# A pre-norm attention and GEGLU block: attention output turned by DMA in bf16, GpSimd's maxima one step later, tangents held by a count, the last steps in pairs

## The chip, the cores and the metric

One core of one Trainium2 chip. The metric is device time in microseconds of one execution. A step-by-step profile of one execution gives the times of single instructions; it has its own time, which is told apart from the median of the runs.

## The reference

```python
x = A_x                                   # 1 x 2048 x 512, bf16
n = layernorm(x)                          # no scale, no shift, eps 1e-5
q, k, v = split(n @ wqkv)                 # 32 heads of 16
p = softmax(q @ k.T * 16 ** -0.5)         # per head, 2048 x 2048
h = x + concat_heads(p @ v) @ wo
m = layernorm(h)
out = h + (gelu_tanh(m @ w_gate) * (m @ w_up)) @ w_down      # F = 1792
```

## The kernel before

Everything is written out by a planner in Python that emits the instructions of each engine in a fixed order; semaphores let the engines run as far ahead as their data allow. Whatever the planner counts (steps, lags, budgets) shapes only that order. Nothing is decided on the chip.

**Units and steps.** The 2048 query rows are cut into 8 groups (`gi`) of 256 rows, the 32 heads into 8 slots of 4 heads. A unit (`ui`) is one group and one slot, so there are 64 (`NU`). Each unit takes 16 steps (`tick`). In a step the first pass (`p1_pair`, L797) computes two score tiles of 128 queries by 512 keys for two heads, and VectorE takes the row maxima of both in one instruction over 1024 columns (`p1_consume`, L806). The second pass runs 24 steps behind (`P2_START`): `p2_tile` (L867) computes the scores again, transposed, 256 keys by 256 queries in one bank, and ScalarE takes the exponential of each bank (`p2_consume`, L879), two in a step, into a ring `PT` of 34 tiles that lie in three tensors (23 in PTM, 4 in PTE, 7 in PTG). The score matmul uses 32 contraction rows of which 16 hold the head; three more rows carry minus the maximum, as three bf16 parts, so that no separate subtraction is needed.

**The maxima on GpSimd.** `negm_part` folds the maxima of key blocks 0 and 1 (at step 8 of a unit, L817 to L819) and of block 2 (at step 12, L821 to L824); `negm_pre` at step 15 folds the last (L832 to L834) and writes the three bf16 parts into ST (to L840). `negm_post` turns ST by a DMA transpose into STG (L846, on SP's queue), and `ADDX` = 4 steps later GpSimd adds STG to QT (L851). Only then may the unit's second pass begin.

**Dense work.** Beside the two passes, class `Dense` hands out pieces of other matmuls, one a step: projections, `item_pv`, `item_ofin`, `item_oproj`, `item_gate`, `item_up`, `item_down`. An item has a bank of its own while it runs; after it the stream pauses for `PAUSE` steps. Gate and up items start only if ScalarE's counted lag is under `LAG_START`. If a step has little dense work, `dummy` (L1285) adds matmuls on constants: two a step while the first pass runs, and up to `FILL_2` per two steps after it.

**Attention output.** `item_pv` (L893) multiplies the exponentials of a unit with V, which has a column of ones, so that 32-row blocks hold 16 outputs and their sum for each of 4 heads, by 256 queries. ScalarE evicts that to OA in fp32. After two units `item_ofin` turns both by four fp32 transposes on TensorE (L919), ScalarE evicts the result to OAT, and GpSimd takes the reciprocal of the sums by a power (`inv`, L928) and multiplies (`mul`, L932) into Otok. When all slots of a group are there, Otok is turned by DMA, projected with wo (`item_oproj`), normalised, turned by DMA again, and the group's FFN goes into the dense stream.

**FFN.** Seven pairs of gate and up items per group. Of the gate's result GpSimd makes the polynomial of the tanh form (L1062 to L1064), ScalarE the tangent (L1055, after `later` has seen a low enough lag), GpSimd the rest (L1060, L1061) and the product with the up part (L1114). `item_down` (L1122) then multiplies with w_down for each half of the group.

**GpSimd's order.** `PoolStream` holds the queued GpSimd work and hands it out within a budget of 1.19 us a step; what is emitted directly is charged by `spend`.

**The end.** After the last first-pass step, 24 second-pass steps remain. They are emitted two steps at a time, four tiles, one exponential for each, with evictions on VectorE (`dve_free`). `tail_a` and `tail_a2` project slots 0 to 5 of the last group in that stretch. `tail_b` then takes the last unit: `tail_norm`, `tail_onT`, the rest of the projection, layer norm, `tail_hnT`, and the FFN of the last group on TensorE, ScalarE and VectorE. `fill` keeps TensorE at work in between, with dense pieces (the down items of group 6 are kept back for it) or with dummies.

Of the kernel before, what the change touches and what calls it, by code (L numbers as in the profile page):

```python
# [222 lines left out]
ADDX = 4  # L223
# [3 lines left out]
FILL_2 = 4  # L227
FILL_LN = 16
LAG_START = 0.4
LAG_OP = 0.2  # L230
TANH_LAG = 2


def bass_sequential_preLN__mha_block__geglu_ffn__prompt_kernel(nc, A_x, A_wqkv, A_wo, B_x, B_w_gate, B_w_up, B_w_down, out):
    dbg = None
    with ExitStack() as es:
# [74 lines left out]
        OAT = at("OAT", [128, 2, 272], FP32)  # L311
# [189 lines left out]
        def startable(it, room):  # L501
            if it[0] is item_gate and par_busy[it[1][1] % 2] and room < 10:
                return False
            if it[0] is item_down and it[1][0] == GL - 1 and not force[0]:
                return False
            if it[0] is item_down and it[1][1] == 0 and not force[0]:
                return not gut_left.get(it[1][0], 0) and dense.now >= gut_last.get(it[1][0], 0) + 1
            return it[0] is not item_projT or not (qks_busy.get(("a", qk_n[0] % 4)) or qks_busy.get(("b", qk_n[0] % 2)))

        class Dense:  # L510
# [17 lines left out]
            def _start(self, item):  # L528
                genfn, a, est, nb = item
                if self.single:  # L530
                    self.bank = banks.take()
                else:
                    self.bank = self.banks[self.rr % len(self.banks)]
                    self.rr += 1
                self.gen = genfn(self.bank, *a)
            def piece(self):
                if self.single and self.pause > 0:
                    return 0
                while True:
# [11 lines left out]
                    try:  # L551
# [42 lines left out]
        class PoolStream:  # L594

            def __init__(self):
                self.q = []
                self.budget = 0.0
            def add(self, ops, then=None):
# [4 lines left out]
            def spend(self, cost):  # L604
                self.budget -= cost
            def run(self, flush=False):
                while self.q and (flush or self.budget >= min(self.q[0][0], 1.0)):
                    if not flush and self.q[0][0] > 2.0 and dense.now % 16 in (1, 2, 3, 13, 14, 15):
                        break
                    cost, fn, then = self.q.pop(0)  # L610
                    self.budget -= cost
                    fn()
# [229 lines left out]
        def negm_post(ui):  # L842
# [10 lines left out]
            defer(ADDX, add)  # L853
# [6 lines left out]
        def p2_tile(ui, j, gp, jj):  # L860
# [3 lines left out]
            m, g, b = j // 2, 2 * gp + jj, banks.take()  # L864
# [5 lines left out]
            return (b, m, g)  # L870

# [10 lines left out]
        def item_pv(b, ui):  # L882
# [18 lines left out]
            evac_act(OA[:, par, 256 * col:256 * col + 256], pbank[:, b, 0:256], [("pb", b)], [("OA", par, col)], cost=0.41)  # L901
            if gi == GL and slot >= NSLOT - 2:
                if col == 0:
                    dense.add(item_ofin, gi, (slot,), front=True, est=3, not_before=dense.now + 3)
            elif col == 1:
                dense.add(item_ofin, gi, (slot - 1, slot), front=True, est=3, not_before=dense.now + 3)
# [6 lines left out]
        oat_busy = {}  # L913
        def item_ofin(b, gi, slots):
            gp, par, ns = gi % 2, slots[0] // 2 % 2, len(slots)
            assert not oat_busy.get(par), "GpSimd too far behind"
            for q in range(2):
                for sp in range(ns):
                    P.op("pe", lambda e, q=q, sp=sp: e.transpose(out=pbank[:, b, 128 * (q * ns + sp):128 * (q * ns + sp) + 128], in_=OA[:, par, 256 * sp + 128 * q:256 * sp + 128 * q + 128], identity=ident32[:]),  # L919
                         reads=[("OA", par, sp), "ident32"], writes=[("pb", b)], sig=(q == 1 and sp == ns - 1))  # L920
                if q == 0 and ns == 2:
                    yield 1
            def norm():
                assert gi < 1 or otok_consumed.get(gi - 1), "dense stream too far behind (Otok reuse)"
                oat4 = OAT[:, par, 0:136 * ns].rearrange("p (q h i) -> p q h i", q=2, i=17)
                li = LINV[:, par, 0:8 * ns].rearrange("p (q h) -> p q h", q=2)
                def inv():
                    P.op("pool", lambda e: e.tensor_tensor(out=li, in0=oat4[:, :, :, 16], in1=negone[:, 0:8 * ns].rearrange("p (q h) -> p q h", q=2), op=ALU.pow),  # L928
                         reads=[("OAT", par), "negone"], writes=[("LINV", par)])
                o_ap = Otok[:, :, 64 * slots[0]:64 * slots[0] + 64 * ns].rearrange("p q (h i) -> p q h i", i=16)  # L930
                def mul():
                    P.op("pool", lambda e: e.tensor_tensor(out=o_ap, in0=oat4[:, :, :, 0:16], in1=li.unsqueeze(3).broadcast_to([128, 2, 4 * ns, 16]), op=ALU.mult),  # L932
                         reads=[("OAT", par), ("LINV", par)], writes=[("Otok", s_) for s_ in slots])
                oat_busy[par] = True
                def over():
                    oat_busy[par] = False
                    slot_done(gi, slots)
                pool.add([(1.45 * ns, inv), (0.31 * ns, mul)], then=over)
            v17 = lambda ap: ap.rearrange("p (qh i) -> p qh i", i=32)[:, :, 0:17]
            evac_act(OAT[:, par, 0:136 * ns].rearrange("p (qh i) -> p qh i", i=17), v17(pbank[:, b, 0:256 * ns]), [("pb", b)], [("OAT", par)], then=norm, cost=0.3)  # L940
            return 1

# [96 lines left out]

        gut_left = {}  # L1040
# [4 lines left out]
        def gelu_chain(par, dE):  # L1045
# [4 lines left out]
            def later(n):  # L1050
                if not force[0] and act_lag[0] > LAG_OP + 0.1 * n:
# [4 lines left out]
                defer(1, second)  # L1056
            def second():
                def done():
# [5 lines left out]
                      o(1.27, lambda e: e.tensor_tensor(out=ts_, in0=ts_, in1=gs, op=ALU.mult), [("th", par), ("g", par)])], then=lambda: defer(TANH_LAG, lambda: later(0)))  # L1064

        def gate_up_mms(b, gi, f, w, nm):
            hT = hnT_l[gi % 2]
            hr = [("hnT", gi % 2, k) for k in range(2)]
# [78 lines left out]
        def tail_a(b):  # L1147
# [9 lines left out]
            dense.add(tail_a2, front=True, est=4, not_before=dense.now + 2)  # L1157
            return 1

        def tail_a2(b):  # L1160
            gp = GL % 2
            for k in range(2):
                for hc in range(3):
                    P.op("pe", lambda e, k=k, hc=hc: e.matmul(pbank[:, k, :], OnT[:, k, hc, :], wo_sb[:, hc, :], start=(hc == 0), stop=False),
                         reads=[("OHa", 0), "wo"], writes=[("pb", k)], sig=False)
                    if hc == 1:
                        yield 2
                P.op("pe", lambda e, k=k: e.matmul(pbank[:, k, :], ident[:], g_h(GL, k), start=False, stop=False),
                     reads=["ident", ("h", gp, k)], writes=[("pb", k)], sig=(k == 1))
                if k == 0:  # L1170
                    yield 2
            a_done[0] = True
            return 2
        a_done = [False]
# [34 lines left out]
        def tail_hnT(b, k):  # L1209
            gp = GL % 2  # L1210
            pt = pbank[:, b, :].bitcast(BF16)
            for dc in range(4):
                P.op("pe", lambda e, dc=dc: e.transpose(out=pt[:, 128 * dc:128 * dc + 128], in_=hn_sb[:, k, 128 * dc:128 * dc + 128], identity=ident[:]),
                     reads=[("OH", k), "ident"], writes=[("pb", b)], sig=(dc == 3))
            o_ap = hnT_l[gp][:, :, 128 * k:128 * k + 128]
            i_ap = pt[:, 0:512].rearrange("p (c s) -> p c s", c=4)
            if k == 1:
                P.op("act", lambda e: e.activation(out=o_ap, in_=i_ap, func=ACT.Copy), reads=[("pb", b)], writes=[("hnT", gp, k)])
            else:
                P.op("dve", lambda e: e.tensor_copy(out=o_ap, in_=i_ap), reads=[("pb", b)], writes=[("hnT", gp, k)])  # L1220
# [6 lines left out]
        def tail_b():  # L1227
            P.op("act", lambda e: e.activation(out=htmp[:, 0:1], in_=nhalf[:, 0:1], func=ACT.Gelu_apprx_tanh), reads=["nhalf"], writes=[("htmp", 0)])
            fill(3)
            while not a_done[0]:  # L1230
                fill(1)
            in_bank(tail_norm)
            fill(3)
# [20 lines left out]
            for k in (0, 1):  # L1254
                in_bank(tail_hnT, k)
            fill(2)
# [6 lines left out]
            for k in range(2):  # L1263
                down_h(k, GL, k)
# [22 lines left out]

        p2_started = False
# [4 lines left out]
        while True:  # L1293
# [11 lines left out]
            dve_free[0] = not p1_ok  # L1305
            dense.tick(tick)
# [100 lines left out]
```

## Time and profile before

| what | us |
|---|---|
| median of 3 runs (lowest, highest) | 1243.94 (1243.86, 1244.21) |
| the profiled execution, its own time | 1243.15 |
| its span | 1241.4 |
| first maximum begins (L806) | 14.66 |
| last maximum begins (L806) | 1183.69 |
| last exponential ends (L879) | 1211.31 |
| last FFN's first gate matmul (L1072) | 1219.97 |

Granted clock of TensorE over the span: 0.997 of full speed. In a profile, PE is TensorE, PEld its weight loads, DVE VectorE, ACT ScalarE, POOL GpSimd, SP the queue that issues DMAs. A line of a group gives line, engine, operation, output and input tiles with shape and count, then the busy time in us, the mean of one in ns, and the idle time just before with what ended it. A line of a timeline gives start, length, engine, line, operation, tiles and how many were merged; in brackets the idle time before it. Instructions on ScalarE and VectorE overlap a little, so the distance from one start to the next (the pitch) is shorter than the duration of one.

Other groups that the change touches, of ScalarE and GpSimd, with shapes kept apart:

```profile
L641 ACT ACTIVATE OA<-pbank 128x256 f32<-128x256 f32 x62 | 24.8, 400 | 0.0
L641 ACT ACTIVATE OAT<-pbank 128x272 f32<-128x272 f32 x31 | 13.1, 422 | 0.0
L1055 ACT ACTIVATE th_sb<-th_sb 128x512 f32<-128x512 f32 x49 | 34.5, 704 | 1.4 <-POOL th_sb L1064 1.4
L851 POOL TENSOR_TENSOR QT<-QT,STG 128x256 bf16<-128x256 bf16 x64 | 42.8, 668 | 19.6 <-DMA STG<-ST 19.4
L821 POOL TENSOR_TENSOR MX<-PM,MX 128x8 f32<-128x8 f32 x64 | 13.0, 203 | 101.5 <-DVE PM L806 101.5
L832 POOL TENSOR_TENSOR MX<-PM,MX 128x8 f32<-128x8 f32 x64 | 12.9, 202 | 163.9 <-DVE PM L806 163.9
```

### The profile page before, as it was taken

The numbers are of one execution on the slowest core, as the hardware profiler recorded it, in microseconds if no ns is written. First come the engines' busy times: TensorE is split into PE (matmuls) and PEld (weight loads), VectorE is DVE, ScalarE is ACT, GpSimd is POOL, SyncE is SP. The second block draws the span as 40 slices with busy tenths as digits, with TensorE's granted clock in tenths as the row PEclk, the third lists the DMA queues.
The fourth block names the chain that finished last, engine by engine and source line by source line (L and its number), as shares of the span: only waits on it lengthen the run. The fifth ranks groups of instructions, "written<-read, shape, count | busy, mean of one in ns | idle before, by whom it ended". The sixth has DMA issues, their size and how long they took to land.

```text
span 1241.4 us, 31438 instructions
## 1 busy us (share of the span) xinstructions
PE 1137.8 (92%) x12680; PEld 437.8 (35%) x12680; DVE 1189.8 (96%) x1088; ACT 1199.9 (97%) x2464; POOL 764.3 (62%) x1540
## 2 busy tenths in 40 slices
PE   7999888899999999999999998999999999999998
PEld 3333222233333333333333333333333333333335
DVE  8999999999999999999999999999999999999923
ACT  7899999999999999999999999999999999999992
POOL 8647774467746765376645777367654766547760
PEclk9999999999999999999999999999999999999989
DMA  5101004300010000100010000100002000100000
GB/s 151 31 22 28 24 19 130 89 6 3 6 31 12 6 6 6 38 5 6 4 27 18 4 6 6 27 17 6 6 4 40 6 4 6 27 19 3 6 13 18
DMA packets 50800, 27.45 MB, mean 22 GB/s; under 512 B 36064, under 2 KB 49632, under 8 KB 50656
## 3 DMA queue, kind: packets, MB, share of 16 engines
q1 hardware_dynamic: 50656, 25.45, 8.0%
q8 instruction: 101, 1.65, 0.5%
q14 instruction: 43, 0.35, 0.1%
HBM read 11.80 MB, written 2.10 MB: 11 GB/s over the span
## 4 chain that ended last, share of the span: by engine, by line
DVE 58%; ACT 30%; PE 9%; POOL 2%; issue 1%; DMA 0%
DVE PM L806 57%; ACT PTM L879 17%; ACT PTG L879 5%; ACT PTE L879 3%; PE pbank L1122 2%; PE pbank L867 2%; PE pbank L797 1%; ACT th_sb L1055 1%; PE pbank L1072 1%; ACT g_sb L641 1%; ACT OnT L1012 1%; ACT u_sb L641 1%; PE pbank L739 1%; PE pbank L998 1%; PE pbank L676 1%
## 5 line engine op out<-in xcount | busy, mean ns | idle before, releaser
L806 DVE TENSOR_REDUCE PM<-pbank 128x2 f32<-128x1024 f32 x1024 | 1162.4, 1224 | 5.3 <-PE pbank L867 2.8
L879 ACT ACTIVATE PTM<-pbank 128x512 bf16<-128x512 f32 x1388 | 737.0, 669 | 4.7
L867 PE MATMUL pbank<-QT,KT 32*128 32x256 bf16 x4096 | 498.2, 273 | 9.7 <-ACT PTM L879 4.4
L797 PE MATMUL pbank<-KT,QT 32*128 32x512 bf16 x2048 | 394.2, 382 | 46.4 <-DVE PM L806 23.6
L1285 PE MATMUL pbank<-ones_bf,ident 128*128 128x512 bf16 x794 | 245.3, 384 | 28.1 <-ACT PTM L879 3.2
L797 PEld LDWEIGHTS pbank<-KT,QT 32*128 32x128 bf16 x2048 | 104.5, 91 | 392.7 <-DVE PM L806 170.3
L879 ACT ACTIVATE PTG<-pbank 128x512 bf16<-128x512 f32 x420 | 228.2, 660 | 1.1 <-PE pbank L867 0.3
L867 PEld LDWEIGHTS pbank<-QT,KT 32*128 32x128 bf16 x4096 | 164.5, 92 | 65.7 <-ACT PTM L879 36.8
L879 ACT ACTIVATE PTE<-pbank 128x512 bf16<-128x512 f32 x240 | 137.7, 667 | 1.9 <-PE pbank L867 1.1
L893 PE MATMUL pbank<-PTM,VA 128*17 128x256 bf16 x2776 | 125.8, 274 | 2.7 <-ACT PTM L879 1.2
L832 POOL TENSOR_TENSOR MX<-PM,MX 128x8 f32<-128x8 f32 x64 | 12.9, 202 | 163.9 <-DVE PM L806 163.9
L1285 PEld LDWEIGHTS pbank<-ones_bf,ident 128*128 128x128 bf16 x794 | 47.6, 97 | 131.4 <-ACT PTM L879 83.8
L928 POOL TENSOR_TENSOR LINV<-OAT,negone 128x16 f32<-128x16 f32 (+1 forms) x32 | 92.7, 2896 | 0.0
L893 PEld LDWEIGHTS pbank<-PTM,VA 128*17 128x17 bf16 x2776 | 60.1, 89 | 46.9 <-issue 29.1
L821 POOL TENSOR_TENSOR MX<-PM,MX 128x8 f32<-128x8 f32 x64 | 13.0, 203 | 101.5 <-DVE PM L806 101.5
L1072 PE MATMUL pbank<-hnT_l,wu_sb 128*128 128x256 bf16 x448 | 67.1, 276 | 3.1 <-ACT PTM L879 0.2
L1072 PE MATMUL pbank<-hnT_l,wg_sb 128*128 128x256 bf16 x448 | 66.9, 275 | 2.5
L1114 POOL TENSOR_TENSOR GUT<-th_sb,u_sb 128x512 bf16<-128x512 f32 x49 | 62.2, 1270 | 5.1 <-DVE u_sb L630 3.0
L1061 POOL TENSOR_TENSOR th_sb<-th_sb,g_sb 128x512 f32<-128x512 f32 x49 | 62.1, 1268 | 4.1
L1064 POOL TENSOR_TENSOR th_sb<-th_sb,g_sb 128x512 f32<-128x512 f32 x49 | 62.1, 1268 | 3.1
L1062 POOL TENSOR_TENSOR th_sb<-g_sb 128x512 f32<-128x512 f32 x49 | 51.0, 1041 | 18.8 <-ACT g_sb L641 18.8
L1122 PE MATMUL pbank<-wd_sb,GUT 128*128 128x512 bf16 x224 | 60.5, 382 | 0.6 <-ACT PTM L879 0.2
(149 smaller groups left out, 1077.3 us busy)
## 6 DMA issues: line engine op xcount, KB each, us to landing
QKS<-QKS SPq DMA_DIRECT2D x27, 112.0 KB, 2.2
x_sb<-in_A_x_dram SPq DMA_DIRECT2D x4, 512.0 KB, 5.6
xres<-in_A_x_dram SPq DMA_DIRECT2D x16, 128.0 KB, 2.2
out_dram<-out_sb SPq DMA_DIRECT2D x16, 128.0 KB, 1.8
wg_sb<-in_B_w_gate_dram SPq DMA_DIRECT2D x4, 448.0 KB, 5.0
wu_sb<-in_B_w_up_dram SPq DMA_DIRECT2D x4, 448.0 KB, 4.0
wd_sb<-in_B_w_down_dram SPq DMA_DIRECT2D x3, 512.0 KB, 6.4
STG<-ST SPq DMA_TRANSPOSE x64, 2.3
```

The source lines that it names most:

```text
L797: P.op("pe", lambda e, g=g, b=b: e.matmul(pbank[:, b, :], QT[32 * g:32 * g + 32, c, slot, 128 * qt:128 * qt + 128], KT[32 * g:32 * g + 32, ...
L806: P.op("dve", lambda e: e.tensor_reduce(out=PM[:, par, qt, kc, g:g + 2], in_=pbank[:, b:b + 2, :], axis=AX.X, op=ALU.max), reads=[("pb", b ...
L867: P.op("pe", lambda e, kt=kt, i=i: e.matmul(pbank[:, b, 256 * i:256 * i + 256], KT[32 * g:32 * g + 32, slot, 128 * kt:128 * kt + 128], QT[ ...
L879: P.op("act", lambda e, b=b, pi=pi: e.activation(out=PTt(pi), in_=pbank[:, b, :], func=ACT.Exp), reads=[("pb", b)], writes=[("PT", pi)], e ...
L893: P.op("pe", lambda e, g=g, kt=kt, pi=pi, i=i: e.matmul(pbank[32 * g:32 * g + 17, b, 0:256], VA[:, kt, 4 * slot + g, :], PTt(pi)[:, 256 * ...
L928: P.op("pool", lambda e: e.tensor_tensor(out=li, in0=oat4[:, :, :, 16], in1=negone[:, 0:8 * ns].rearrange("p (q h) -> p q h", q=2), op=ALU ...
L1061: o(1.27, lambda e: e.tensor_tensor(out=ts_, in0=ts_, in1=gs, op=ALU.mult), [("th", par), ("g", par)])], then=done)
L1064: o(1.27, lambda e: e.tensor_tensor(out=ts_, in0=ts_, in1=gs, op=ALU.mult), [("th", par), ("g", par)])], then=lambda: defer(TANH_LAG, lamb ...
L1072: P.op("pe", lambda e, dc=dc, fc=fc, i=i: e.matmul(pbank[:, b, 256 * i:256 * i + 256], w[:, dc, 128 * fc:128 * fc + 128], hT[:, dc, :], st ...
L1114: P.op("pool", lambda e: e.tensor_tensor(out=o_ap, in0=shp(ts_), in1=shp(us), op=ALU.mult), reads=[("th", par), ("u", par)], writes=o_keys ...
L1122: P.op("pe", lambda e: e.matmul(pbank[:, b, :], GUT[:, fc, 128 * k:128 * k + 128], wd_sb[:, fc, :], start=first, stop=last), reads=[("GUT" ...
L1285: P.op("pe", lambda e: e.matmul(pbank[:, b, :], ident[:], ones_bf[:, 0:512], start=True, stop=True), reads=["ident", "ones_bf"], writes=[( ...
```

## The change

- The attention output of a unit is evicted to OB in bf16, turned by a DMA transpose on SP's queue (`o_turn`), and normalised by GpSimd five steps later, one unit at a time (`o_norm`). Only slot 6 of the last group still goes through TensorE (`item_ofin`); slot 7 is treated in `tail_norm` as before.
- GpSimd's folds of the maxima are emitted one step later (9, 13, and the beginning of the next unit's step 0), and the add into QT one step earlier (`ADDX` 3).
- A tangent is emitted only when a count of GpSimd's time (`pool.t`) says that its polynomial is done, and at a lower lag of ScalarE; gate and up items start at a lower lag; the reciprocal is kept out of slightly other steps.
- After the first pass, exponentials are taken over two banks at a time where the two ring places are neighbours (`p2_pair`), with bank pairs that rotate; dense items start with no pause there; `FILL_2` is 5; the first down item of group 6 may run there.
- `tail_a2` is emitted in `tail_b`, half before and half after `tail_norm`, in place of two fills; the second half of the layer norm's transposes is evicted in two pieces by two engines; evictions in `tail_b` are ScalarE's; `FILL_LN` is 13, and the first matmuls into the last output banks come earlier.

```diff
-ADDX = 4
+ADDX = 3
-FILL_2 = 4
-FILL_LN = 16
-LAG_START = 0.4
+FILL_2 = 5
+FILL_LN = 13
+LAG_START = 0.3
+POLY = 0.2
+LAG_TH = 0.2
...
-            if it[0] is item_down and it[1][0] == GL - 1 and not force[0]:
+            if it[0] is item_down and it[1] == (GL - 1, 1) and not force[0]:
...
-                            self.pause = PAUSE
+                            self.pause = 0 if dve_free[0] else PAUSE
...
-                    if not flush and self.q[0][0] > 2.0 and dense.now % 16 in (1, 2, 3, 13, 14, 15):
+                    if not flush and self.q[0][1].__name__ == 'inv' and dense.now % 16 in (1, 2, 3, 12, 13, 14):
                         break
                     cost, fn, then = self.q.pop(0)
                     self.budget -= cost
+                    self.t = max(self.t, 1.135 * dense.now) + 1.08 * cost
...
-            defer(ADDX, add)
+            defer(ADDX + (ui == NU - 1), add)
...
+        def p2_pair(ui, tiles):
...
+            (b0, b1), (q0, q1) = [t[0] for t in tiles], pis
+            assert b1 == b0 + 1
+            if q1 == q0 + 1 and pt_tiles[q0][0] is pt_tiles[q1][0]:
+                o_ap = pt_tiles[q0][0][:, pt_tiles[q0][1]:pt_tiles[q0][1] + 2, :]
+                P.op("act", lambda e: e.activation(out=o_ap, in_=pbank[:, b0:b0 + 2, :], func=ACT.Exp), reads=[("pb", b0), ("pb", b1)], writes=[("PT", q0), ("PT", q1)])
+            else:
+                for b, pi in ((b0, q0), (b1, q1)):
+                    P.op("act", lambda e, b=b, pi=pi: e.activation(out=PTt(pi), in_=pbank[:, b, :], func=ACT.Exp), reads=[("pb", b)], writes=[("PT", pi)])
...
-            evac_act(OA[:, par, 256 * col:256 * col + 256], pbank[:, b, 0:256], [("pb", b)], [("OA", par, col)], cost=0.41)
...
+                evac_act(OB[:, ui % 2, :], pbank[:, b, 0:256], [("pb", b)], [("OB", ui % 2)], cost=0.27, then=lambda: o_turn(ui))
...
+            P.dma("sp", lambda e: e.dma_start_transpose(out=OBT[:, par, :, :], in_=OB[:, par, :]), ("obT", par), reads=[("OB", par)], writes=[("OBT", par)])
+            o4 = OBT[:, par].rearrange("p q (g i) -> p q g i", i=32)
+            defer(5, lambda: o_norm(gi, slot, par, o4, ("OBT", par), ob_busy))
...
+            pool.add([(1.45, inv), (0.31, mul)], then=over)
...
-                if not force[0] and act_lag[0] > LAG_OP + 0.1 * n:
+                if not force[0] and (act_lag[0] + (0.48 if dense.gen is not None and dense.cur in (item_gate, item_up) else 0) > LAG_TH + 0.1 * n or poly_end[par] > 1.135 * dense.now + POLY):
                     defer(1, lambda: later(n + 1))
                     return
...
+            def poly_done():
+                poly_end[par] = pool.t
+                defer(TANH_LAG, lambda: later(0))
...
         def tail_b():
+            dve_free[0] = False
             P.op("act", lambda e: e.activation(out=htmp[:, 0:1], in_=nhalf[:, 0:1], func=ACT.Gelu_apprx_tanh), reads=["nhalf"], writes=[("htmp", 0)])
-            fill(3)
             while not a_done[0]:
                 fill(1)
+            tail_a2(0)
             in_bank(tail_norm)
-            fill(3)
+            tail_a2(1)
             in_bank(tail_onT)
...
             fill(FILL_LN)
-            for k in (0, 1):
-                in_bank(tail_hnT, k)
-            fill(2)
+            sp_ = [b for b in range(2, 8) if b not in (own, other)]
+            tail_hnT(sp_[0], 0, (0, 1, 2, 3), "dve")
+            tail_hnT(sp_[1], 1, (0, 1), "act")
+            tail_hnT(sp_[2], 1, (2, 3), "dve")
+            for k in range(2):
+                down_h(k, GL, k)
...
+        def unit_end(ui):
+            pool.spend(1.8)
+            negm_pre(ui)
+            negm_post(ui)
...
+            if tick and tick % 16 == 0 and p1_ok:
+                unit_end(tick // 16 - 1)
             dense.tick(tick)
...
                 if tick == 16 * NU:
-                    for b_ in (2, 3):
-                        banks.give(b_)
-                for d_ in (0, 1):
-                    for jj in (0, 1):
-                        t2l.append(p2_tile((t2 + d_) // 16, (t2 + d_) % 16, 1 - (tick + d_) % 2, jj))
-                        p2_consume((t2 + d_) // 16, t2l)
-                        t2l = []
+                    own = dense.bank if dense.gen is not None else banks.free[0]
+                    other = own ^ 1
+                    banks.free = [other] if dense.gen is not None else [own, other]
+                    pairs = [0, 2, 10 - (own & 6)]
+                for d_ in ((0, 1) if t2 + 1 < 16 * NU else (0,)):
+                    b_ = pairs.pop(0)
+                    pairs.append(b_)
+                    ui_, j_ = (t2 + d_) // 16, (t2 + d_) % 16
+                    p2_pair(ui_, [p2_tile(ui_, j_, 1 - (tick + d_) % 2, jj, b_ + jj) for jj in (0, 1)])
...
-                if tick % 16 in (8, 12):
+                if tick % 16 in (9, 13):
                     pool.spend(0.7)
-                    negm_part(tick // 16, 1 if tick % 16 == 8 else 2)
-                if tick % 16 == 15:
-                    pool.spend(1.8)
-                    negm_pre(tick // 16)
-                    negm_post(tick // 16)
+                    negm_part(tick // 16, 1 if tick % 16 == 9 else 2)
+                if tick == 16 * NU - 1:
+                    unit_end(tick // 16)
```

More of the change, by code (lines that the diff above doesn't have):

```diff
@@ L611, in run @@
                     self.budget -= cost
+                    self.t = max(self.t, 1.135 * dense.now) + 1.08 * cost
                     fn()
@@ L911, in bass_sequential_preLN__mha_block__geglu_ffn__prompt_kernel @@
         P2_START = 16 + LAGX
[L913 to L916, printed above, removed]
-            for q in range(2):
[L918 to L938, printed above, removed]
@@ L939, in item_ofin @@
+        def item_ofin(b, gi):
+            slot = NSLOT - 2
+            for q in range(2):
+                P.op("pe", lambda e, q=q: e.transpose(out=pbank[:, b, 128 * q:128 * q + 128], in_=OA[:, 1, 128 * q:128 * q + 128], identity=ident32[:]),
+                     reads=[("OA", 1, 0), "ident32"], writes=[("pb", b)], sig=(q == 1))
             v17 = lambda ap: ap.rearrange("p (qh i) -> p qh i", i=32)[:, :, 0:17]
[L940 removed]
+            evac_act(OAT[:].rearrange("p (qh i) -> p qh i", i=17), v17(pbank[:, b, 0:256]), [("pb", b)], ["OAT"],
+                     then=lambda: o_norm(gi, slot, 1, OAT[:].rearrange("p (q h i) -> p q h i", q=2, i=17), "OAT", {}), cost=0.3)
@@ L1156, in tail_a, with tail_a2 @@
             P.op("dve", lambda e: e.tensor_copy(out=OnT[:, :, 0:3, :], in_=pt[:, 0:768].rearrange("p (k c s) -> p k c s", k=2, c=3)), reads=[("pb", b)], writes=[("OHa", 0), ("OH", 0), ("OH", 1)])
-            dense.add(tail_a2, front=True, est=4, not_before=dense.now + 2)
+            a_done[0] = True
             return 1
-        def tail_a2(b):
+        a_done = [False]
+        def tail_a2(k):
             gp = GL % 2
[L1162 to L1174, printed above, removed]
+            for hc in range(3):
+                P.op("pe", lambda e, hc=hc: e.matmul(pbank[:, k, :], OnT[:, k, hc, :], wo_sb[:, hc, :], start=(hc == 0), stop=False),
+                     reads=[("OHa", 0), "wo"], writes=[("pb", k)], sig=False)
+            P.op("pe", lambda e: e.matmul(pbank[:, k, :], ident[:], g_h(GL, k), start=False, stop=False),
+                 reads=["ident", ("h", gp, k)], writes=[("pb", k)], sig=False)
         def fill(n):
```

70 lines of the change are left out of this document (51 added, 19 removed).

## The prediction, made before the changed kernel ran

> **What bounds the kernel now.** I read, in order, the page's busy shares, the groups of VectorE, VectorE's timeline, and then ScalarE, VectorE and GpSimd from 1184 us on.
>
> Shares and the costliest VectorE group:
>
> ```profile
> PE 1137.8 (92%) x12680; PEld 437.8 (35%) x12680; DVE 1189.8 (96%) x1088; ACT 1199.9 (97%) x2464; POOL 764.3 (62%) x1540
> L806 DVE TENSOR_REDUCE PM<-pbank 128x2 f32<-128x1024 f32 x1024 | 1162.4, 1224 | 5.3 <-PE pbank L867 2.8 <-PE pbank L797 1.5
> ```
>
> Three engines look full, but only one has an interval of its own to obey. The 1024 maxima (one a step) take 1162.4 us, and VectorE sat idle before them for 5.3 us in all. Between the first steps and the last maximum nothing but fewer or shorter maxima could save much, and the change leaves their number and shape alone. VectorE's timeline around the end of a group shows what can be saved:
>
> ```profile
> 661.23 5.75 DVE L806 TENSOR_REDUCE PM<-pbank 128x2 f32<-128x1024 f32 x5 [0.29 <-PE pbank L867]
> 667.16 139.52 DVE L806 TENSOR_REDUCE PM<-pbank 128x2 f32<-128x1024 f32 x123 [0.17 <-PE pbank L867]
> ```
>
> A group of 128 steps loses 0.29 + 0.17 = 0.46 us, at the same place each time, where ScalarE takes L1005, L1012 and an output eviction close together; six groups make 2.8 us. A step is 139.52 / 123 = 1.134 us.
>
> So the gain has to come from behind the last maximum, which ends at 1183.69 + 1.24 = 1184.93 us: 56.5 us of the 1241.4. ScalarE there:
>
> ```profile
> 1184.72 3.08 ACT L879 ACTIVATE PTG<-pbank 128x512 bf16<-128x512 f32 x6
> 1187.61 7.05 ACT L879 ACTIVATE PTM<-pbank 128x512 bf16<-128x512 f32 x14
> ...
> 1202.95 0.60 ACT L879 ACTIVATE PTE<-pbank 128x512 bf16<-128x512 f32 x1 [1.10 <-PE pbank L867]
> 1203.45 1.57 ACT L879 ACTIVATE PTG<-pbank 128x512 bf16<-128x512 f32 x3
> 1205.33 2.06 ACT L879 ACTIVATE PTG<-pbank 128x512 bf16<-128x512 f32 x4 [0.31 <-PE pbank L867]
> 1207.25 4.06 ACT L879 ACTIVATE PTM<-pbank 128x512 bf16<-128x512 f32 x8
> ```
>
> The last 48 exponentials run at a pitch of (7.05 - 0.60) / 13 = 0.49 us and end at 1211.31. 48 x 0.49 = 23.5 us of 26.6; the rest is two tangents (1.1 us) and some 1.6 us of waiting for TensorE. The table of 2 us stretches says why TensorE is late:
>
> ```profile
> 1198.00:1200.00 2.00, 1.46 (x9) 0.40 (x10) 0.00 (x0) 2.00 (x5) 1.92 (x3) 0.83 0.01 4
> 1200.00:1202.00 2.00, 2.00 (x7) 0.51 (x6) 0.00 (x0) 1.86 (x4) 2.00 (x2) 0.50 0.00 0
> 1202.00:1204.00 2.00, 2.00 (x12) 0.57 (x12) 0.00 (x0) 1.05 (x3) 1.99 (x2) 0.50 0.00 0
> 1204.00:1206.00 2.00, 2.00 (x14) 0.71 (x13) 0.00 (x0) 1.69 (x5) 0.40 (x1) 0.50 0.00 0
> ```
>
> The fourth number is ScalarE's busy time, the sixth TensorE's granted clock, in the order TensorE, weight loads, VectorE, ScalarE, GpSimd, clock. After stretches with TensorE 1.3 to 1.5 us busy of 2 the clock is 0.50 for some 6 us, and ScalarE falls to 1.05 us of 2. Behind the exponentials comes a chain of short steps to 1219.97 (output, projection, layer norm, transposes), then the last group's FFN on TensorE to the end.
>
> **The parts of the change and their cost.**
>
> *The attention output.* Removed: 31 paired turns on TensorE (L919, 27 us of its busy time) and 31 evictions OAT by ScalarE, each 1182.26 - 1181.98 = 0.28 us of pitch, 8.7 us in 1140. Neither sets the step: VectorE does, so I count 0. What is left of OA's eviction keeps its size (256 columns, pitch 1178.08 - 1177.81 = 0.27); in bf16 it may cost the same. Added: 62 transposes by DMA of the size of STG<-ST, 2.3 us from issue to landing. The reader comes 5 steps later, 5 x 1.134 = 5.7 us, so they are hidden with 3.4 us over for the eviction itself. On SP's queue the new transpose waits for ScalarE's eviction some four steps before the turn of the maxima (L846) is issued, and that one is what would be late next; SP now stands up to 17.2 us at L846 waiting for ST alone, so the queue has room. If that cover went, QT would be late: it has about 4 us before its second pass begins. On GpSimd:
>
> ```profile
> L928 POOL TENSOR_TENSOR LINV<-OAT,negone 128x16 f32<-128x16 f32 x31 | 91.0, 2937 | 0.0
> L928 POOL TENSOR_TENSOR LINV<-OAT,negone 128x8 f32<-128x8 f32 x1 | 1.7, 1652 | 0.0
> ```
>
> Two halves cost 2 x 1.652 against 2.937, and the products 2 x 0.403 against 0.622: 31 x 0.55 = 17 us more on an engine idle for 477. Hidden, 0.
>
> *Maxima a step later.* GpSimd waits 163.9 / 63 = 2.6 us at L832 and 101.5 / 59 = 1.7 at L821, because it arrives early. One step later takes up to 1.1 us off each. The add into QT (L851) is emitted a step earlier, so it will wait more than its present 19.4 us: seven short steps (2.0 us) plus 2.3 of DMA lie before it. What is queued behind it is the FFN's products. Gains and losses here are of one size, and the add still ends about 3 to 4 steps before TensorE needs it. 0, bounds +-0.5.
>
> *Lower lag limits, tangents that wait for GpSimd's count.* No instruction added. Fewer evictions and lower limits should thin the bunching on ScalarE that makes the 0.46 us a group; bounds 0 to -2.8, and a loss of the same size if the FFN's work bunches elsewhere. I take half the gain, -1.4. They can also delay the FFN of group 6; that is a rival below.
>
> *The last 48 exponentials in pairs.* Ring places go up from 28 (the six PTG above), so of 24 pairs two straddle a tile border and stay single: 22 pairs, 4 singles. No 1024-column exponential is in the trace. Nearest row: two 1024-column copies in ScalarE's timeline,
>
> ```profile
> 21.66 1.94 ACT L487 ACTIVATE xnT<-pbank 128x1024 bf16<-128x1024 bf16 x2 [0.62 <-PE pbank L485]
> ```
>
> pitch 1.94 - 1.02 = 0.92 against 2 x 0.49 = 0.98. Saved 22 x 0.06 = 1.3 us. Evictions say the same: 256 columns more cost 0.49 - 0.27 = 0.22, so a wide one 0.49 + 0.44 = 0.93. Bounds: 0 if the wait for both halves eats it; 22 x 0.18 = 4.0 if all that a single eviction takes beside its columns were saved (0.39 for 256 and 0.60 for 512 leave 0.18). I take 1.3, by the row of the same width. The Trainium skill, "ScalarE: Activation LUTs", section "What ACT_TABLE_LOAD costs", has back-to-back activations overlapping by about 93 ns of a fixed 186, so a merge would save 93 ns: 2.0 us by that, an estimate. The trace's 0.49 pitch is shorter than that rule gives, so I stay with the rows.
>
> *Clock and ballast in that stretch.* FILL_2 goes from 4 to 5: one more 512-column matmul (0.22 us at full clock) per two steps. TensorE then has 8 scores (0.56) and 5 x 0.22 = 1.1, that is 1.66 of 1.84 us, 90%; now it is 1.42 of 1.96, 72%. Dense items start with no pause there, and L1164/L1168 (8 matmuls, 5 us at the half clock) leave the stretch. I count 1.2 of the 1.6 us of waiting; bounds: 1.6 saved, or 1.6 lost if the clock falls twice.
>
> *The end.* The eight matmuls now stand around tail_norm in place of two fills of three: 2 x 0.22 = 0.4 us more on TensorE, of which 0.2 to 0.3 beside VectorE's eviction and reciprocal. Three fills fewer before the transposes: they started at 1218.44 though hn was ready at 1217.88, -0.5. The second half is evicted in two pieces by two engines rather than 0.60 on ScalarE: about -0.3. Down rows of group 6: the first is let into the exponentials' stretch, the second (15 matmuls) just fills what is left to fill. Sum -0.5, bounds -1.2 and +0.5. The last FFN (1219.97 to 1238.4) is untouched.
>
> Sum: -1.4 - 1.3 - 1.2 - 0.5 = -4.4. The profiled execution took 1243.15 (span 1241.4), the median of the runs is 1243.94; 1243.94 - 4.4 = 1239.5.
>
> **Rivals.**
>
> *Nothing to measure.* The clock falls again in the stretch, since TensorE now waits for two banks at a time; then the pairs wait for TensorE as the singles did, and the group stalls stay. For it: 72% busy was enough to lose the clock. Against: the ballast. Only the end is left, with a little of the pairs: 1243.94 - 0.5 - 0.5 = 1243. The Trainium skill, "TensorE: Matmul & The Clock Gate", section "A second HAM failure mode: psum-queue depth-cycling", describes micro-idles between groups of matmuls that make the clock swing; the 0.50 above, with no idle over 0.9 us, agrees.
>
> *Slower: the FFN of group 6 comes late.* Its last product (L1114) ends at 1207.52 + 1.27 = 1208.8, and the down rows start at 1211.69, a margin of 2.9 us. A tangent may now be held until GpSimd's count and ScalarE's lag both allow it. If each of the seven is held one step longer and the chains are serial, 7 x 1.134 = 7.9 us, 5 past the margin. Then ballast fills the layer norm, and 30 down matmuls (30 x 0.22 = 6.5 us) stand behind it on TensorE alone, less the 4.4 from above and with part of a chain of products exposed (1.27 + 0.6): 1243.94 + 6.5 + 1.9 - 4.4 = about 1248. It decides once the last product ends later than about 8 us behind the last exponential, less beyond the first down row. Against: 31 dense items and 8.7 us of ScalarE are gone, so the FFN gets more steps, not fewer.
>
> *More than forecast.* All six group stalls go (-2.8), the FFN of group 6 is over before the stretch (no tangents, -1.1), no waiting (-1.6), pairs -1.3, end -1.0: -7.8, 1236.
>
> *The change does not do what it says*: pairs that mostly split. The ring count above rules it out.
>
> **How the numbers follow.** Forecast 0.54, more 0.13, nothing 0.16, slower 0.17. About 0.2% (2.5 us, so below 1241.4 or above 1246.4) is what a measurement of this kernel can tell from no change. Of the forecast's 0.54, 0.03 fall within it. Faster 0.51 + 0.13 = 0.64; same 0.03 + 0.16 = 0.19; slower 0.17. The forecast's own range is 1237 to 1242; the whole range reaches into the two outer cases, 1235.0 to 1246.0, leaving out some 0.04 below and 0.14 above.
>
> **What would show it.** Right: the last maximum within 2 us of 1184.9 or earlier; in the 24 us behind it 22 exponentials of 128x1024 at a pitch near 0.92, ScalarE idle under 0.5 us, granted clock 1.0; gate matmuls of the last FFN some 0.5 us sooner behind the last exponential. Wrong: more idle time before the maxima; a product of group 6 later than the last exponential; clock 0.5 in the end; a wide exponential near 0.98.

## The result, and the profile after

The changed kernel takes 1256.41 us (median of 4 runs, 1253.97 to 1258.46) against 1243.9 before: 1.0099 times as long, 95% interval 1.0087 to 1.0111. It is 12.5 us slower; 4.4 us faster was forecast. The profiled execution of after is the quickest of its four, 1253.97 us with a span of 1252.2.

The page of after, shares and costliest group; then, by form, the two halves of the normalisation (line, engine, operation, tiles; busy us, mean ns; idle before and its end):

```profile
PE 1121.6 (90%) x12632; PEld 421.4 (34%) x12632; DVE 1188.8 (95%) x1086; ACT 1195.5 (95%) x2414; POOL 779.3 (62%) x1602
L814 DVE TENSOR_REDUCE PM<-pbank 128x2 f32<-128x1024 f32 x1024 | 1163.0, 1213 | 16.7 <-PE pbank L875 13.7 <-PE pbank L805 1.6
```

```profile
L952 POOL TENSOR_TENSOR LINV<-OBT,negone 128x8 f32<-128x8 bf16 x62 | 103.5, 1669 | 1.1 <-DMA OBT<-OB 1.1
L859 POOL TENSOR_TENSOR QT<-QT,STG 128x256 bf16<-128x256 bf16 x64 | 42.8, 669 | 127.6 <-DMA STG<-ST 127.6
```

The maxima cost what they did, but VectorE now idles 16.7 us before them, 13.7 of it behind the second pass's scores (L875, formerly L867). GpSimd waits 1.1 us in all for the new transposes, and 127.6 us for the turned maxima where it waited 19.4.

By stages, from the profiles' timelines (us; "first gate" is the first Gelu evaluation of the last FFN):

| kernel | last maximum ends | last exponential ends | first gate | span |
|---|---|---|---|---|
| before | 1184.9 | 1211.3 (+26.4) | 1221.0 (+9.7) | 1241.4 |
| after | 1197.3 | 1220.6 (+23.3) | 1231.9 (+11.3) | 1252.2 |
| e3, maxima back | 1186.9 | 1210.7 (+23.8) | 1222.0 (+11.3) | 1242.4 |
| e9, tangents 3 steps behind | 1187.0 | 1210.4 (+23.4) | 1219.3 (+8.8) | 1239.6 |
| e10, best | 1186.3 | 1209.3 (+23.0) | 1218.1 (+8.8) | 1238.4 |
| e11, count told of the wait | 1187.3 | 1210.4 (+23.1) | 1221.7 (+11.3) | 1242.0 |

Against before, after loses 12.4 us before the last maximum, gains 3.1 in the exponentials, loses 1.6 up to the last FFN: +10.9, which is the difference of the spans (10.8, by unrounded times).

The stretch of the last exponentials, ScalarE's timeline of after:

```profile
1200.28 4.82 ACT L892 ACTIVATE PTM<-pbank 128x1024 bf16<-128x1024 f32 x5
1205.17 0.63 ACT L1087 ACTIVATE th_sb<-th_sb 128x512 f32<-128x512 f32 x1
1205.71 5.58 ACT L892 ACTIVATE PTM<-pbank 128x1024 bf16<-128x1024 f32 x6
...
1216.66 3.92 ACT L892 ACTIVATE PTM<-pbank 128x1024 bf16<-128x1024 f32 x4
```

No waits are left there, and a wide exponential has a pitch of (1211.13 - 1205.71) / 6 = 0.90 us, 1211.13 being the start of the next activation. The 2 us stretches (TensorE, weight loads, VectorE, ScalarE, GpSimd busy; granted clock) stay at clock 1.0:

```profile
1206.00:1208.00 2.00, 1.86 (x19) 0.78 (x17) 0.38 (x2) 2.00 (x3) 1.92 (x3) 1.00 0.00 0
1208.00:1210.00 2.00, 1.98 (x17) 0.76 (x17) 0.49 (x2) 2.00 (x3) 2.00 (x2) 1.00 0.00 0
```

So the end's first part does what was forecast. The loss lies ahead of it. VectorE's, ScalarE's and GpSimd's timelines of after around one of the two longest stops:

```profile
269.48 1.23 DVE L814 TENSOR_REDUCE PM<-pbank 128x2 f32<-128x1024 f32 x1 [2.09 <-PE pbank L875]
270.96 1.23 DVE L814 TENSOR_REDUCE PM<-pbank 128x2 f32<-128x1024 f32 x1 [0.25 <-PE pbank L875]
272.48 57.98 DVE L814 TENSOR_REDUCE PM<-pbank 128x2 f32<-128x1024 f32 x51 [0.29 <-PE pbank L875]
```

```profile
260.75 4.16 ACT L904 ACTIVATE PTM<-pbank 128x512 bf16<-128x512 f32 x8
267.02 0.63 ACT L1087 ACTIVATE th_sb<-th_sb 128x512 f32<-128x512 f32 x1 [2.11 <-POOL th_sb L1099]
267.56 2.04 ACT L904 ACTIVATE PTM<-pbank 128x512 bf16<-128x512 f32 x4
269.46 0.41 ACT L649 ACTIVATE OB<-pbank 128x256 bf16<-128x256 f32 x1
```

```profile
260.24 0.23 POOL L848 TENSOR_TENSOR ST<-R,ST 128x8 bf16<-128x8 f32 x1
262.90 0.67 POOL L859 TENSOR_TENSOR QT<-QT,STG 128x256 bf16<-128x256 bf16 x1 [2.43 <-DMA STG<-ST]
263.53 0.40 POOL L956 TENSOR_TENSOR Otok<-OBT,LINV 128x128 bf16<-128x128 bf16 x1
263.89 1.04 POOL L1097 TENSOR_TENSOR th_sb<-g_sb 128x512 f32<-128x512 f32 x1
265.02 0.62 POOL L1098 TENSOR_SCALAR th_sb<-th_sb 128x512 f32<-128x512 f32 x1
265.72 1.26 POOL L1099 TENSOR_TENSOR th_sb<-th_sb,g_sb 128x512 f32<-128x512 f32 x1
```

Read from below: the maxima's parts are written (L848) and the add (L859) comes straight behind, so GpSimd stands 2.43 us for the DMA. The polynomial queued behind it ends at 266.98. ScalarE's tangent had been placed for GpSimd on time; ScalarE stands 2.11 us, the exponentials behind the tangent free no bank, TensorE's order stops at the second pass, and VectorE loses 2.09 us. There are eight such waits of ScalarE in the table of waits of after (us in total, times, longest):

```profile
ACT th_sb L1087 <- POOL th_sb L1099: 9.7, 8, 2.3
```

Two of the eight are of this size, the other six take 0.74 to 1.13 us. The stops of VectorE right after each add up to 10.6 of its 13.7 us; before the change all its stops there made 2.8.

### The profile page after: what moved, and what is told of

Its sections match the earlier page's. It is cut to its first block, busy times and chain, and to the rows that moved or that the text cites. A ratio compares the mean times of both kernels' runs of the same rounds, so it can differ in the third digit from the quotient of the medians.

```text
span 1252.2 us, 31428 instructions
## 1 busy us (share of the span) xinstructions
PE 1121.6 (90%) x12632; PEld 421.4 (34%) x12632; DVE 1188.8 (95%) x1086; ACT 1195.5 (95%) x2414; POOL 779.3 (62%) x1602
## 4 chain that ended last, share of the span: by engine, by line
ACT 39%; DVE 36%; PE 10%; POOL 9%; DMA 3%; issue 3%; POOLq 0%
DVE PM L814 36%; ACT PTM L904 21%; ACT PTG L904 7%; ACT PTE L904 4%; DMA STG<-ST 2%; PE pbank L1157 2%; PE pbank L805 2%; ACT th_sb L1087 2%; PE pbank L1107 2%; POOL th_sb L1097 1%; PE pbank L1317 1%; PE pbank L875 1%; ACT g_sb L649 1%; POOL th_sb L1099 1%; ACT u_sb L649 1%
## 5 line engine op out<-in xcount | busy, mean ns | idle before, releaser
L814 DVE TENSOR_REDUCE PM<-pbank 128x2 f32<-128x1024 f32 x1024 | 1163.0, 1213 | 16.7 <-PE pbank L875 13.7
L904 ACT ACTIVATE PTM<-pbank 128x512 bf16<-128x512 f32 x1357 | 724.6, 686 | 8.0 <-PE pbank L875 1.8
L875 PE MATMUL pbank<-QT,KT 32*128 32x256 bf16 x4096 | 484.7, 273 | 19.4 <-ACT PTM L904 6.9
L805 PE MATMUL pbank<-KT,QT 32*128 32x512 bf16 x2048 | 395.0, 384 | 45.2 <-DVE PM L814 23.1
L1317 PE MATMUL pbank<-ones_bf,ident 128*128 128x512 bf16 x870 | 262.5, 384 | 40.9 <-ACT PTM L904 11.1
L904 ACT ACTIVATE PTG<-pbank 128x512 bf16<-128x512 f32 x407 | 223.7, 668 | 3.4 <-PE pbank L875 1.9
L875 PEld LDWEIGHTS pbank<-QT,KT 32*128 32x128 bf16 x4096 | 159.1, 92 | 66.9 <-ACT PTM L904 32.1
L859 POOL TENSOR_TENSOR QT<-QT,STG 128x256 bf16<-128x256 bf16 x64 | 42.8, 669 | 127.6 <-DMA STG<-ST 127.6
L952 POOL TENSOR_TENSOR LINV<-OBT,negone 128x8 f32<-128x8 bf16 x62 | 103.5, 1669 | 1.1 <-DMA OBT<-OB 1.1
L1317 PEld LDWEIGHTS pbank<-ones_bf,ident 128*128 128x128 bf16 x870 | 50.3, 97 | 156.3 <-ACT PTM L904 100.0
L829 POOL TENSOR_TENSOR MX<-PM,MX 128x8 f32<-128x8 f32 x64 | 13.0, 203 | 67.2 <-DVE PM L814 66.7
```

The costliest lines, as they stand in the source:

```text
L805: P.op("pe", lambda e, g=g, b=b: e.matmul(pbank[:, b, :], QT[32 * g:32 * g + 32, c, slot, 128 * qt:128 * qt + 128], KT[32 * g:32 * g + 32, ...
L814: P.op("dve", lambda e: e.tensor_reduce(out=PM[:, par, qt, kc, g:g + 2], in_=pbank[:, b:b + 2, :], axis=AX.X, op=ALU.max), reads=[("pb", b ...
L875: P.op("pe", lambda e, kt=kt, i=i: e.matmul(pbank[:, b, 256 * i:256 * i + 256], KT[32 * g:32 * g + 32, slot, 128 * kt:128 * kt + 128], QT[ ...
L904: P.op("act", lambda e, b=b, pi=pi: e.activation(out=PTt(pi), in_=pbank[:, b, :], func=ACT.Exp), reads=[("pb", b)], writes=[("PT", pi)], e ...
L952: P.op("pool", lambda e: e.tensor_tensor(out=li, in0=o4[:, :, :, 16], in1=negone[:, 0:8].rearrange("p (q h) -> p q h", q=2), op=ALU.pow), ...
L1317: P.op("pe", lambda e: e.matmul(pbank[:, b, :], ident[:], ones_bf[:, 0:512], start=True, stop=True), reads=["ident", "ones_bf"], writes=[( ...
```

## The experiments

**Theory A**: tangents are emitted before GpSimd has their polynomial, since it is late by its wait before the add. **Theory B**: the lower lag limits and the tangent rule bunch ScalarE's work. **Theory C**: the new transposes crowd the queues. All ratios are to the kernel before, with 95% intervals. Where only one constant is shown, it is the whole edit.

*e1*, after with

```diff
-ADDX = 3
+ADDX = 4
```

> The changed kernel with the add into QT emitted four steps after the maxima's end instead of three (ADDX 4), nothing else. Theory A (the add stands at the head of GpSimd's queue waiting for the turn of the maxima, the polynomials behind it come late, ScalarE stops at a tangent that was emitted too early, and no bank comes free for the second pass): GpSimd's wait before the add falls from 127.6 us to some 60 to 80, ScalarE's wait for the polynomial from 9.7 to under 3, VectorE's idle time before the maxima from 16.7 to 6 to 9, time 1245 to 1249. Theory B (the lower lag limits and the new rule for tangents bunch ScalarE's work, whatever GpSimd does): idle before the maxima stays at 14 or more, time 1252 to 1259. Theory C (the 62 new transposes crowd the DMA queues): as B.

1256.87 us, 1.0105 (1.009 to 1.012). GpSimd's wait before the add fell only to 113.9 us; ScalarE's stayed, 9.1, and so did the time. By the numbers of the time this is B's; but the edit did not take away the wait that A blames, so it decides nothing.

*e2*, after with

```diff
-TANH_LAG = 2
+TANH_LAG = 4
```

> The changed kernel with tangents emitted two steps later behind their polynomial (TANH_LAG 4 in place of 2); the order on GpSimd up to the add is the same. Theory A: GpSimd still waits 127 us before the add, but ScalarE no longer for the polynomial (9.7 to under 1 us), VectorE's idle time before the maxima falls to 5 to 7, time 1242 to 1247, a little of it given back by a later FFN of group 6. Theory B: the same tangents in the same neighbourhood of evictions, idle time 12 or more, time 1252 or more. Theory C: as B.

1248.7 us, 1.0043 (1.0026 to 1.006). GpSimd waits 147.7 us before the add, more than ever, yet VectorE idles 5.4 us before the maxima, and the last maximum ends at 1185.0. B and C, which had 12 us or more there, fall with that. The time is above A's range because the FFN of group 6 came late: 18.15 us from the last exponential to the first gate.

*e3*, after with the old places of the maxima (ADDX 4 as well)

```diff
-                if tick % 16 in (9, 13):
+                if tick % 16 in (8, 12):
...
-                if tick == 16 * NU - 1:
-                    unit_end(tick // 16)
+                if tick % 16 == 15:
+                    pool.spend(1.8)
+                    negm_pre(tick // 16)
+                    negm_post(tick // 16)
```

> The changed kernel with the maxima's folds back at steps 8, 12 and 15 and the add four steps later, as before the change. Theory A: GpSimd waits under 30 us before the add, ScalarE under 2 us for polynomials, idle before the maxima 5 to 7 us, time 1241 to 1245. Theory B and theory C: 1252 or more, with idle before the maxima above 12.

1244.98 us, 1.0013 (1.0004 to 1.0022); GpSimd's wait before the add 49.6, idle before the maxima 7.8, both somewhat above what A expected. Of the loss this one part carries 11.4 us.

*e4*, before with only that part (the reverse edit, ADDX 3)

> The kernel before with only the maxima's folds one step later and the add one step earlier, nothing else of the change. Theory A: GpSimd waits 100 us or more before the add, ScalarE some 5 to 15 us for polynomials, idle before the maxima rises from 5.3 to 12 to 20, time 1249 to 1258. Theory B and theory C: no tangent rule and no new transposes here, so 1243 to 1245.

1293.8 us, 1.0407 (1.0391 to 1.0422), outside every range. GpSimd's wait (137.9), ScalarE's (37.0) and VectorE's idle time (23.8 us) are A's, only larger. But 40 us lie between the last exponential and the first gate: four tangents of group 6 run there, from 1237.5 to 1261.3. The planner's own order had become late, with four pairs of gate and up behind the second pass. The time is the sum of both.

*e5*, after with ADDX 6

> The changed kernel with the add into QT emitted six steps after the maxima's end instead of three (ADDX 6). With four steps GpSimd's wait before the add fell only to 113.9 us, because the 1.8 us charged for the maxima leave GpSimd's budget empty for most of two steps, so little stood between. By the planner's order the first down item of group 6 now starts at step 1038, inside the last exponentials. Theory A (GpSimd late by its wait before the add, ScalarE stopped at tangents): GpSimd's wait before the add under 60 us, ScalarE's for polynomials under 3, idle before the maxima 5 to 8 us, time 1239 to 1244. Theory B (lower lag limits and the tangent rule bunch ScalarE) and C (new transposes crowd the queues): idle still above 12, time 1249 or more.

1248.37 us, 1.0043 (1.0028 to 1.0058); its profile is of the longest of its four runs, 1250.82 us. GpSimd's wait fell to 33.9 us, ScalarE's waits for polynomials are gone, as A has it; but VectorE still idles 14.2 us. Once TensorE waits 2.4 us for the add itself, which now comes too late, and 20-odd stops of about 0.3 us remain, whose cause stays open. A later add is no cure.

*e6*, e3 with

```diff
-... ((act_lag[0] <= LAG_START or force[0] or ...
+... ((act_lag[0] <= LAG_START or dve_free[0] or force[0] or ...
```

> The maxima back at steps 8, 12 and 15 with the add four later, and gate and up items free to start after the first pass whatever ScalarE's counted lag (evictions are VectorE's there). By the planner's order up item 6 of group 6 starts at step 1026 instead of 1038, and its first down item at 1038 instead of behind the exponentials. If the 1.6 us that the end lost is the 15 down matmuls behind the layer norm (15 x 0.216 = 3.2 us), the time from the last exponential to the first gate of the last FFN falls from 11.3 to about 8.0 us, and the time to 1241 to 1243. If it is the order of the projection and the evictions, it stays at 11.3 and the time at 1244 to 1246.

1242.35 us, 0.9987 (0.9977 to 0.9996). Last exponential to first gate: 8.8 us instead of 11.3. The late down matmuls were the end's loss.

*e9*, after with TANH_LAG 3

> The changed kernel with tangents three steps behind their polynomial (TANH_LAG 3 in place of 2), nothing else; the maxima stay one step later. By the planner's order the down item starts at step 1038. Theory A: three steps are 3.4 us, GpSimd is late by some 2.5, so ScalarE's wait for polynomials falls from 9.7 to under 2 us, idle before the maxima to 5 to 7, time 1239 to 1243. Theory B: idle above 12, time above 1250.

1241.93 us (1241.08 to 1246.63), 0.9997 (0.9985 to 1.0009). One constant takes back 14.5 us of the median: GpSimd waits 134.8 us before the add, ScalarE 1.4 for polynomials, VectorE idles 7.3. The down item starts early as well.

*e10*, e6 with TANH_LAG 3

> The kernel of the down item's early start (maxima back in their old steps) with tangents three steps behind. Theory A: the few waits of ScalarE that are left go as well, last maximum within 1 us of 1184.9, the 48 exponentials in 23.3 us, 8.0 from the last of them to the last FFN: 1238.5 to 1240.5, faster than both kernels. If group stalls remain for another reason: 1240.5 to 1243.

1240.58 us (1240.01 to 1241.97), 0.9977 (0.9968 to 0.9986): faster than both kernels. That is just above A's range, and the last maximum is 1.4 us later than before the change where A had it within 1, so some stops have another reason.

*e11*, after with

```diff
         def add():
+                pool.t = max(pool.t, 1.135 * dense.now) + 2.4
                 pool.spend(0.7)
```

> The changed kernel (maxima one step later, add after three steps, TANH_LAG 2) in which only the count of GpSimd's time that tangents wait for is told of the wait before the add: 2.4 us are charged to the count when the add is emitted. GpSimd's own order hardly changes. Theory A (tangents are emitted before GpSimd has their polynomial, because the count leaves out the wait for the DMA before the add): ScalarE's wait for polynomials falls from 9.7 to under 2 us, idle before the maxima to 5 to 8, time 1241 to 1246, with the 3.2 us of late down matmuls still in the end. If the count is not where it fails (the order of the other evictions is): ScalarE's wait stays above 6 and the time above 1250.

1242.97 us, 0.9992 (0.9982 to 1.0001). ScalarE waits 1.7 us for polynomials, VectorE idles 8.2 before the maxima. GpSimd still waits 128.2 us before the add:

```profile
POOL QT L860 <- DMA STG<-ST: 128.2, 63, 4.4
ACT th_sb L1088 <- POOL th_sb L1100: 1.7, 2, 1.2
```

The same tangent as above, ScalarE's and GpSimd's timelines of e11 (its lines stand one lower):

```profile
261.23 6.32 ACT L905 ACTIVATE PTM<-pbank 128x512 bf16<-128x512 f32 x12
267.43 0.39 ACT L649 ACTIVATE OB<-pbank 128x256 bf16<-128x256 f32 x1
267.70 0.64 ACT L1088 ACTIVATE th_sb<-th_sb 128x512 f32<-128x512 f32 x1
```

```profile
263.38 0.67 POOL L860 TENSOR_TENSOR QT<-QT,STG 128x256 bf16<-128x256 bf16 x1 [2.43 <-DMA STG<-ST]
...
266.20 1.27 POOL L1100 TENSOR_TENSOR th_sb<-th_sb,g_sb 128x512 f32<-128x512 f32 x1
```

GpSimd stands the same 2.43 us, but the tangent now follows four more exponentials and OB's eviction, and finds its input done (267.47). This shows the cause: not GpSimd's wait, but that the planner's count did not know of it.

*e12*, e10 with the last 48 exponentials one bank at a time

```diff
-            if q1 == q0 + 1 and pt_tiles[q0][0] is pt_tiles[q1][0]:
+            if False:
```

> The best kernel so far (maxima in their old steps, tangents three steps behind, early down item) with the last 48 exponentials taken one bank at a time, in the same bank pairs and order. If pairs are worth 22 x 0.06 to 0.08 us: the time from the last maximum to the last exponential grows from 23.0 to 24.3 to 24.8 us, time 1241.5 to 1242.5. If ballast and order did it and ScalarE was not the bound: no more than 0.4 us.

1242.29 us, 0.9986 (0.9977 to 0.9996). From the last maximum (1186.03) to the last exponential (1210.42) 24.4 us instead of 23.0.

*e13*, e10 with FILL_2 4

> The best kernel so far with FILL_2 at 4 in place of 5. If the ballast keeps the granted clock at 1.0 through the last exponentials: here the clock falls to 0.5 for some 4 to 7 us as before the change, ScalarE waits 1 to 2 us for TensorE, time 1241.5 to 1242.5. If TensorE is busy enough without it (bank pairs, no long projection in between): clock 1.0 and within 0.3 us of 1240.6.

1240.16 us (1239.78 to 1241.69), 0.9973 (0.9961 to 0.9984); the stretch takes 23.0 us as with 5. The stretch of e13 in which TensorE was thinnest while ScalarE still had exponentials to take, and two behind it:

```profile
1194.00:1196.00 2.00, 1.17 (x24) 0.37 (x24) 0.00 (x0) 2.00 (x4) 1.92 (x3) 1.00 0.08 28
1198.00:1200.00 2.00, 1.76 (x17) 0.71 (x16) 0.62 (x2) 2.00 (x3) 1.22 (x2) 1.00 0.00 0
1200.00:1202.00 2.00, 1.69 (x14) 0.62 (x10) 0.00 (x0) 2.00 (x5) 1.92 (x2) 1.00 0.04 8
```

The clock stays at 1.0 even behind the stretch with 1.17 us of 2: the extra ballast is not what keeps it there.

*e14*, e10 with LAG_START 0.4 and the old condition for tangents, `act_lag[0] > LAG_OP + 0.1 * n`

> The best kernel so far with the old lag limits and the old rule for tangents (LAG_START 0.4, no count, no allowance for a running gate or up item), still three steps behind. If the lower limits thin the bunching on ScalarE, as forecast at 1.4 us: idle before the maxima rises from 6 to 7 or 8 us, time 1241.5 to 1243. If they were worth nothing: 1240 to 1241.

1245.76 us, 1.0016 (1.0007 to 1.0025), with the last maximum at 1191.5 instead of 1186.3. The lower limits and the count's rule are worth 5.2 us in this order, more than expected. Idle time before the maxima shows 2.2 of them (8.2 us against 6.0); the other 3 lie in the time of the maxima themselves (1166.1 against 1163.0), and why is open.

## Why the prediction was wrong

**The step that failed** is "Maxima a step later", taken at 0 with bounds of 0.5 either way. It saw that the add would wait more than its 19.4 us (127.6 now), and that "what is queued behind it is the FFN's products", and stopped there. Behind those stands ScalarE's tangent, in the same order as the exponentials that free TensorE's banks. Followed on, at the stop shown 2.4 us of GpSimd were 2.1 of ScalarE and 2.1 of VectorE; the eight places together are 9.7 us of ScalarE and 10.6 of VectorE. The balance "gains and losses here are of one size" was about right for GpSimd's waiting (143 us less at the three folds, 108 more at the add), and beside the point: a wait for the maxima in the old place came ahead of the work that the planner timed, the new one came in the middle of it. e3 puts 11.4 us on this part, e11 and e9 show that it acts through the tangents.

**The rival of the slower side** had the right instruction and the wrong sign: it feared tangents held too long. They were let go too early, since the rule that holds them leaves the DMA's wait out.

**The first down item of group 6.** "The first is let into the exponentials' stretch" did not happen: the last up item of that group (number 6) came late, its product ends at 1212.60 + 1.27 = 1213.9, and the down item stood behind the layer norm. The limit on ScalarE's counted lag had held the up item: e6 lifts only that against e3, and the end shrinks from 11.3 to 8.8 us. ScalarE's and TensorE's timelines of after:

```profile
1228.22 2.54 PE L1157 MATMUL pbank<-wd_sb,GUT 128*128 128x512 bf16 x11
...
1230.81 1.04 PE L1107 MATMUL pbank<-hnT_l,wg_sb 128*128 128x256 bf16 x8
```

Gates wait behind these down matmuls: 28 of them, 6.7 us, lie between 1220.5 and 1231.0, where e10 has 14, 3.35 us, in its like stretch. The end came out at +1.6 instead of -0.5; with the item early (e6, e9, e10) it is 8.8 - 9.7 = -0.9.

**Right:** the pairs, 22 wide and 4 single as counted, 1.3 us forecast, 24.4 - 23.0 = 1.4 by e12. The Trainium skill, "ScalarE: Activation LUTs", section "What ACT_TABLE_LOAD costs", would have made it 2.0, an estimate; the rows were nearer. The stretch as a whole, 2.5 forecast (1.3 and 1.2), 3.1 measured; but the credit to FILL_2 was wrong (e13), and the eight projection matmuls had taken 2 x (1.46 + 0.63) = 4.2 us there, not 5. That it is the projection moved out of the stretch and the bank pairs that keep the clock was not tried alone. The attention output was hidden, as forecast: OB's eviction has OA's length (392 ns against 400), GpSimd's extra work is 103.5 + 25.0 + 1.6 + 0.4 - 112.4 = 18 us against 17, and neither theory C nor any wait speaks against it; but no run leaves this part alone out.

**Lower lag limits:** -1.4 forecast. e14 gives 5.2 us for them within the new order, but against before nothing was won: e10's last maximum is at 1186.3, before's at 1184.9, with 3.0 and 2.8 us of stops behind the second pass. What else in the new order costs what the limits take back was not separated.

## What to carry to other kernels

When an instruction that waits for a DMA is moved in an in-order queue, follow every chain behind it to the engine that sets the pace; totals of waiting on the moved engine say nothing. A planner's clock that places work on another engine has to be charged for waits, not only for work, and here a step of slack (e9) cost less than being early. A filler or early item is only worth its price once the planned order shows that it starts where it was meant to.

## What was not expected of the hardware

TensorE's clock fell after one stop of little more than 2 us. TensorE's timeline of after, and the stretches around 266 to 274 us:

```profile
268.19 0.39 PE L875 MATMUL pbank<-QT,KT 32*128 32x256 bf16 x2 [2.29 <-ACT PTM L904]
```

```profile
266.00:268.00 2.00, 0.00 (x0) 0.00 (x0) 1.40 (x2) 0.98 (x2) 1.92 (x3) 1.00 0.00 0
268.00:270.00 2.00, 1.71 (x26) 0.75 (x26) 0.52 (x1) 2.00 (x6) 1.91 (x4) 1.00 0.04 8
270.00:272.00 2.00, 2.00 (x16) 0.70 (x16) 1.75 (x2) 1.85 (x4) 1.92 (x4) 0.50 0.16 33
272.00:274.00 2.00, 2.00 (x18) 0.67 (x12) 1.62 (x3) 1.57 (x5) 1.74 (x6) 0.65 0.00 0
```

TensorE stands still for 2.29 us, and some 2 us later it runs at half clock for about 3 us, when its steps take 1.5 us (first-pass scores at 270.31, 271.83 and 273.34) instead of 1.13, which costs VectorE 0.25 and 0.29 us more. The Trainium skill, "TensorE: Matmul & The Clock Gate", section "What's actually happening", has the half rate after at least one idle window of about 3.4 us; here 2.29 were enough, and in e9 a stop of 1.35 us was followed by a clock of 0.69 and 0.50 in the next two stretches. The length of a stop alone does not tell: behind the six stops of the changed kernel that cost VectorE 0.70 to 1.23 us the clock stayed at 1.0, and in the kernel before it fell near 1200 us with no idle time over 0.9 us. A stop followed by half clock costs more than its length. Over the four runs of after the mean clock goes from 0.997 to 0.990 as the span goes from 1252.2 to 1256.7 us; in e9 three of ten runs, at a mean clock of 0.996, took 1246 us, the others, at 0.998 or 0.999, 1241 to 1242.
